# First queries through the casting queue, group 3 transposed by TensorE, part of a normalisation moved to ScalarE, and the last store in halves: a windowed attention with a SwiGLU block on one core

## The chip, the core and the metric

The kernel runs on one core of a Trainium2 chip. The metric is the device time of one execution in microseconds; the median of 14 executions of the kernel before is 250.9 us (249.39 to 252.73).

## What is computed

Batch 4, 8 heads, 768 positions, head size 64; 4 sink positions and a window of 128. The attention output, heads side by side (512 wide), goes through a gated feed-forward block of inner width 1536. All inputs and the output are float32 in HBM.

```python
scores = scale * np.matmul(q, k.transpose(0, 1, 3, 2))
keep = is_sink | in_window          # pos < 4, or 0 <= query - key < 128
scores = np.where(keep, scores, -1000000000.0)
a = softmax(scores)                 # exp over its row sum
x = np.matmul(a, v)                 # then (B, S, H*D) -> 3072 x 512
g = x @ w_gate
out = (g * sigmoid(g) * (x @ w_val)) @ w_out
```

## The kernel before, in words

**Groups and blocks.** The 3072 tokens are cut twice. Attention works in 12 groups g of 256 tokens, three for each batch entry. The feed-forward block works in 8 token blocks tb of 256 or 512 tokens: `SIZES = [256, 256, 256, 512, 512, 512, 512, 256]`. Groups 0, 1, 2 are blocks 0, 1, 2; groups 3 and 4 are block 3, and so on.

**Loading.** Keys, queries, values and weights are read through POOL's DMA queue, which casts float32 to bf16 on the way. POOL has eight completion semaphores for it and uses them in turn, so a DMA on POOL waits until the one eight places before it has landed. `load4(g)` (L96) loads a group with four tokens in a partition row, keys in partitions 0 to 63, queries in 64 to 127, one DMA each. `load1(g)` (L107) loads it with one token in a row, in four DMAs. The buffers `nat` are four. Group 0 has its own code: two casting DMAs for halves of the keys (L169), and the queries as float32 in four DMAs (L173), two each from ACT's and SP's queues, into staging tiles `st`.

**From tokens to columns.** The score matmuls need keys and queries with head size on the partitions. Groups below `NPE = 3` are transposed by PE (`transpose`, L257, matmuls with an identity of the same type; an ACT copy brings the keys and a DVE copy the queries from PSUM, L263). The others are transposed by two DMA transpositions on SP's queue (`cross_T`, L285), from `nat` to the tile kqT.

**One group's attention.** `step_S(g, p2)` does the scores of four heads (PE L323), exponentials on ACT (L330), and the mask by a DVE multiplication (L335). `step_K` does the sink scores for groups that aren't the first of their batch entry. `step_PV(g, j, hh)` does half of the heads of one 128-token tile j (PE L370) with a column of ones that gives the row sums, then a reciprocal (L375) and the product xn on DVE (L382); with `act` the product is made by four ACT operations (L378). `step_X(g, j)` transposes xn by PE (L406) into xT, evicted by DVE (L412) or ACT (L410). From group 5 on (`NXPE`) SP's DMA transposes xn instead (L388).

**The feed-forward units.** `gate(tb, f)` computes pg and pv (L434, eight matmuls of 256 columns or four of 512 each), tanh on ACT (L441), then u and ht on DVE (L447, L448). `down(tb, ts)` accumulates 12 matmuls (L462) for 128 tokens, evicts them on ACT with a factor of 0.5 (L466), and SP stores them (L468).

**The order** is written by hand. After a start for group 0, in which `warm(n)` fills PE with matmuls on zeros (L235), `weave(us, slots)` walks a list of feed-forward units and calls the attention steps that a table puts in each. In the first list, units 0 to 13 are the gates of blocks 0 and 1 and one down, 14 to 19 the gates of block 2, and 20 to 24 the remaining downs of blocks 0 to 2:

```python
us = [g0[0], (alone, 0, 0), *g0[1:4], *g1, *g0[4:6], downs(0)[0], *g2,
      downs(0)[1], *downs(1), *downs(2)]
```

Inside a gate unit the steps come between pg and pv. DVE work of a step is put off in a list `later` and issued by `flush` at the unit's end, or where the table says flush. Each engine works through its instructions in the order issued. T(g), Ss(g), K(g), PVs(g), Xs(g) in the table are the steps named above; C(g) is `cross_T(g)`, and T and C end by issuing the loads of group g + 4. `sinks(b)` copies the sink keys of a batch entry (L295) and builds its sink values (L300).

Of the kernel before, what the change touches and what calls it, by code (L numbers as in the profile page):

```python
# [8 lines left out]
FP32 = mybir.dt.float32  # L9
# [6 lines left out]
def kernel(  # L16
# [26 lines left out]
    SIZES = [256, 256, 256, 512, 512, 512, 512, 256]  # L43
    assert sum(SIZES) == NTOK and NG == 12 and S == 768
    OFF = [sum(SIZES[:i]) for i in range(len(SIZES))]
    NPE = 3
    NXPE = 5
    VS = 72
    FCH = [2, 2, 2, 2, 4]
# [30 lines left out]
    def bank(shape, dtype, name):  # L80
        return psum.tile(shape, dtype, tag="b", name=name)
# [4 lines left out]
    def four_tokens(src, g, hs):  # L86

        b, c = divmod(g, GC)
        return src[b, hs, c * 256:(c + 1) * 256].rearrange(
            "h (m r) d -> m h (r d)", r=4)  # L90

    def load4(g):

        x = natp.tile([P, H, 4 * D], BF16, tag="kq", name="kq")
        for i, src in ((0, k), (1, q)):
            nc.gpsimd.dma_start(  # L96
                x[64 * i:64 * (i + 1)], four_tokens(src, g, slice(0, H)))
        nat[g] = x

    def load1(g):  # L100

        b, c = divmod(g, GC)
        x = natp.tile([P, 2, 2, H * D], BF16, tag="kq", name="kq")
        for j in range(2):
            t0 = c * 256 + j * P
            for i, src in ((0, k), (1, q)):
                nc.gpsimd.dma_start(  # L107
                    x[:, j, i].rearrange("p (h d) -> p h d", d=D),
                    src[b, :, t0:t0 + P].rearrange("h m d -> m h d"))
        nat[g] = x  # L110
# [44 lines left out]
        ks = const.tile([P, NP2 * KS], BF16, tag=f"ks{b}", name="ks")  # L155
        kss.append(ks)


    nc.vector.memset(ident, 0.0)
    id32 = const.tile([P, P], FP32)  # L160
    nc.vector.memset(id32, 0.0)
    wm = const.tile([P, 512], BF16)
    nc.vector.memset(wm, 0.0)
    wake = const.tile([P, 1], FP32)
    nc.vector.memset(wake, 0.0)
    nat[0] = natp.tile([P, H, 4 * D], BF16, tag="kq", name="kq")
    for k2 in range(2):
        hs = slice(4 * k2, 4 * k2 + 4)
        nc.gpsimd.dma_start(nat[0][0:64, hs], four_tokens(k, 0, hs))  # L169
    first = []  # L170
    for p in range(NP2):
        st = opool.tile([P, 2, 4 * D], FP32, tag="ot", name="st")
        (nc.scalar, nc.sync)[p % 2].dma_start(  # L173
            st[64:P], four_tokens(q, 0, slice(2 * p, 2 * p + 2)))
        first.append(st)
    make_identity(nc, ident, nomemset=True)
    make_identity(nc, id32, nomemset=True)
    load_v(0)
    load_gate(0)

# [7 lines left out]
    for ks in kss:  # L188
        nc.vector.memset(ks, 0.0)
    nc.vector.memset(diag_h, 1.0)  # L190


    nc.gpsimd.iota(tq, [[1, P]], base=0, channel_multiplier=0,
                   allow_small_or_imprecise_dtypes=True)
    nc.gpsimd.iota(tk, [[0, 1]], base=0, channel_multiplier=1,
                   allow_small_or_imprecise_dtypes=True)
    dh = diag_h.rearrange("q (p h) -> q p h", h=2)
    nc.gpsimd.affine_select(
        out=dh, in_=dh, compare_op=ALU.is_ge, fill=0.0, base=0,
# [31 lines left out]
    def warm(n):  # L231

        ps = bank([P, 512], FP32, "wm")
        for _ in range(n):
            nc.tensor.matmul(ps, ident, wm, start=True, stop=True)  # L235

    def step_T(g, ph):

        if ph == 0:
            new_kq(g)  # L240
        own = lambda i, p: nat[g][:, 2 * p:2 * p + 2]
        transpose(g, ph, own, (ident, ident))

    def new_kq(g):
        kTs[g] = kqtp.tile([P, NP2, 256], BF16, tag="kT", name="kT")
        qTs[g] = kqtp.tile([P, NP2, 256], BF16, tag="qT", name="qT")

    def transpose(g, ph, rows, ids):


        pts = [bank([P, 2, 64, 4], FP32, "pt") for _ in range(2)]
        for p in range(2):
            for r in range(4):
                for h in range(2):
                    for i in range(2):
                        o = slice(64 * i, 64 * (i + 1))
                        nc.tensor.matmul(  # L257
                            pts[i][64 * h:64 * (h + 1), p, :, r],
                            rows(i, 2 * ph + p)[o, h, r * D:(r + 1) * D],
                            ids[i][o, o], start=True, stop=True)  # L260
        for i, (dst, copy) in enumerate(((kTs, nc.scalar.copy),
                                         (qTs, nc.vector.tensor_copy))):
            copy(out=dst[g][:, 2 * ph:2 * ph + 2],  # L263
                 in_=pts[i].rearrange("q a m r -> q a (m r)"))
# [42 lines left out]
    def step_S(g, p2):  # L307

        b, c = divmod(g, GC)
        if p2 == 0:  # L310
            e_t[g] = epool.tile([P, H, 512], BF16, tag="e", name="e")

        parts = [(2 * c, 0, 2, P), (2 * c + 1, 1, 1, 3 * P)]
        if c > 0:
            parts.insert(0, (2 * c - 1, 0, 1, 0))
        lo = 0 if c > 0 else P
        pss = [bank([P, 512], FP32, "s") for _ in range(4)]
        for pp in range(2):
            p = 2 * p2 + pp
            for t, j, n, col in parts:  # L320
                for h in range(2):
                    r = slice(h * D, (h + 1) * D)
                    nc.tensor.matmul(  # L323
                        pss[2 * pp + h][:, col:col + n * P], keys(b, t, r, p),
                        queries(g, r, p, j, n), start=True, stop=True)
        m = (mask if c > 0 else mask0).rearrange("q (o a) x -> q o (a x)", o=1)
        for pp in range(2):
            h0 = 4 * p2 + 2 * pp
            for h in range(2):
                nc.scalar.activation(  # L330
                    e_t[g][:, h0 + h, lo:512], pss[2 * pp + h][:, lo:512],
                    AF.Exp, scale=scale)

            def dve(e=e_t[g][:, h0:h0 + 2, lo:512]):
                nc.vector.tensor_tensor(  # L335
                    e, e, m[:, :, lo:512].broadcast_to([P, 2, 512 - lo]), op=ALU.mult)
            later.append(dve)
# [80 lines left out]
    def gate(tb, f, attn):  # L418
# [30 lines left out]
            hts[tb][:, f:f + two].rearrange("p a n -> p (a n)"), u, pv, op=ALU.mult)  # L449
        flush()  # L450

    def down(tb, ts, attn):
        po = bank([P, DM], FP32, "pd")
        n = DFC // 4
        at = {}
        for i, a in enumerate(attn):
            at.setdefault(DFC * (i + 1) // (len(attn) + 1), []).append(a)
        for f in range(DFC):
            for a in at.get(f, []):
                a()  # L460
                flush()
            nc.tensor.matmul(  # L462
                po, hts[tb][:, f, ts * P:(ts + 1) * P], wos[f // n][:, f % n],
                start=(f == 0), stop=(f == DFC - 1))
        ot = opool.tile([P, DM], FP32, tag="ot", name="ot")
        nc.scalar.activation(ot, po, AF.Copy, scale=0.5)  # L466
        r0 = OFF[tb] + ts * P
        nc.sync.dma_start(out[r0:r0 + P], ot)  # L468
# [9 lines left out]
    def downs(tb):  # L478
        return [(down, tb, t) for t in range(SIZES[tb] // P)]
# [56 lines left out]


    new_kq(0)
    warm(10)
    for ph in range(2):  # L540
        transpose(0, ph, lambda i, p: first[p] if i else nat[0][:, 2 * p:2 * p + 2],
                  (ident, id32))
    build_masks()
    step_S(0, 0)
    warm(2)
    step_S(0, 1)
# [16 lines left out]
    for i in range(4):  # L563
        load_out(i)
    for g in (3, 4):
        load1(g)
        load_v(g)


    g0, g1, g2 = gates(0), gates(1), gates(2)  # L570
    us = [g0[0], (alone, 0, 0), *g0[1:4], *g1, *g0[4:6], downs(0)[0], *g2,
          downs(0)[1], *downs(1), *downs(2)]
    weave(us, slots(
        (0, T(1)), (1, Ss(1) + [K(1)]), (3, PVs(1) + [flush]),
        (4, [A(step_X, 1, 0), A(step_X, 1, 1, True), flush]),
        (8, T(2)), ((9, 10), Ss(2)), (10, [K(2)]), (10, C(3)),
        (11, PVs(2)[:2] + [flush]), (12, PVs(2)[2:] + [flush]),
        (13, [A(step_X, 2, 0), A(step_X, 2, 1, True), flush]), (13, C(4)),
        ((16, 17), Ss(3)), (18, sinks(1)), ((18, 18, 19, 19), PVs(3)),
        (20, Xs(3)), ((20, 21), Ss(4)), (21, [K(4)]),  # L580
        (22, C(5)), ((22, 22, 23, 23), PVs(4)), (24, Xs(4))))

    def pair(ga, gb, sh=0):
        s = sh
# [46 lines left out]
```

## Time and profile before

| | |
|---|---|
| median of 14 executions | 250.9 us |
| the profiled execution | 250.02 us |
| its span | 248.3 us |
| PE busy | 234.0 us (94%) |
| DVE busy | 161.1 us (65%) |
| ACT busy | 110.9 us (45%) |
| POOL busy | 68.7 us (28%) |
| software DMA queue, share of 16 engines' span | 69.2% |
| hardware DMA queue of SP | 25.3% |
| last matmul ends, last eviction ends | 244.4 us, 245.1 us |

The times in the views are microseconds from the start of the span. A line of a timeline gives start, length, engine, source line, operation, output<-inputs and a count; a bracket gives the idle time of the engine just before it and what ended it. A busy PE is not always PE doing needed work: the filler matmuls wm count as busy. Transfers show twice, as the issuing instruction on POOL or SP and as DMA time until the data have landed.

### The profile page before, as it was taken

Reading aid. Unit: us, or ns where it says so; the run is one execution under the profiler, and the core shown is the slowest. Engines: PE = TensorE matmul, PEld = TensorE weight load, DVE = VectorE, ACT = ScalarE, POOL = GpSimd, SP = SyncE. Lnnn points to the kernel's source line nnn. Section 1 sums busy time; section 2 is a strip of 40 time slices with the busy share of each in tenths; the row PEclk is TensorE's granted clock in tenths of the full one; section 3 lists DMA queues with packets and bytes.
Section 4 is the critical chain, followed back from the end, with each engine's and each line's share of the span. In section 5 each row is a group of like instructions: output and inputs, shape, how many; then the busy total and the mean of one; then the engine's idle time right before and its main releaser. Section 6 shows DMA issues by size and latency. Waiting matters only on the chain.

```text
span 248.3 us, 5061 instructions
## 1 busy us (share of the span) xinstructions
PE 234.0 (94%) x2011; PEld 133.4 (54%) x2011; DVE 161.1 (65%) x339; ACT 110.9 (45%) x219; POOL 68.7 (28%) x90
## 2 busy tenths in 40 slices
PE   4979899999699999999999999999999999999993
PEld 1557687777545444544445454445454445488441
DVE  2478978948954388892398981298980389878000
ACT  2478338437162266542665711555612662232121
POOL 8965373954694088005200000000000000000000
PEclk9999999999999999999999999999999999999999
DMA  7999999999999999759960264600244200200122
GB/s 135 170 185 199 202 192 183 145 122 153 180 154 198 164 243 156 38 67 171 207 110 0 44 87 124 173 3 1 48 82 127 84 3 0 42 3 0 61 111 84
DMA packets 102775, 27.63 MB, mean 111 GB/s; under 512 B 89952, under 2 KB 99680, under 8 KB 102752
## 3 DMA queue, kind: packets, MB, share of 16 engines
q0 software_dynamic: 71936, 13.90, 69.2%
q1 hardware_dynamic: 30528, 13.15, 25.3%
q10 hardware_dynamic: 288, 0.26, 0.5%
q8 instruction: 16, 0.26, 0.4%
q14 instruction: 7, 0.06, 0.1%
HBM read 28.34 MB, written 6.29 MB: 139 GB/s over the span
## 4 chain that ended last, share of the span: by engine, by line
PE 65%; DMA 17%; DVE 9%; POOL 4%; issue 2%; ACT 0%; DVEq 0%; POOLq 0%; ACTq 0%; SPq 0%
PE pd L462 24%; PE pv L434 18%; PE pg L434 16%; DMA kq<-in_k_dram 5%; DMA kq<-in_q_dram 5%; DMA kqT<-kq 4%; PE o L370 4%; DMA wv<-in_moe_w_val_dram 3%; PE s L323 3%; DVE ht L448 3%; DVE e L335 2%; DVE u L447 2%; DVE xn L382 1%; POOL kq L107 1%; POOL va L123 1%
## 5 line engine op out<-in xcount | busy, mean ns | idle before, releaser
L434 PE MATMUL pv<-xT,wv 128*128 128x256 bf16 (+1 forms) x384 | 74.3, 326 | 1.3 <-DVE ht L448 1.1
L434 PE MATMUL pg<-xT,wg 128*128 128x256 bf16 (+1 forms) x384 | 74.2, 326 | 0.8 <-DVE xT L412 0.6
L441 ACT ACTIVATE th<-pg 128x512 f32<-128x512 f32 x72 | 43.4, 606 | 64.8 <-PE pg L434 64.4
L447 DVE SCALAR_TENSOR_TENSOR u<-th,pg 128x512 bf16<-128x512 f32 x72 | 49.1, 682 | 31.1 <-ACT th L441 30.7
L462 PE MATMUL pd<-wo,ht 128*128 128x512 bf16 x288 | 66.5, 379 | 0.0
L448 DVE TENSOR_TENSOR ht<-u,pv 128x512 bf16<-128x512 bf16 x72 | 49.5, 687 | 10.2 <-PE pv L434 3.3
L434 PEld LDWEIGHTS <-wg 128*128 128x128 bf16 x384 | 37.3, 98 | 27.0 <-issue 1.0
L330 ACT ACTIVATE e<-s 128x512 bf16<-128x512 f32 (+1 forms) x96 | 46.0, 581 | 6.7 <-PE s L323 6.6
L434 PEld LDWEIGHTS <-wv 128*128 128x128 bf16 x384 | 34.7, 98 | 21.2 <-issue 3.1
L462 PEld LDWEIGHTS <-ht 128*128 128x128 bf16 x288 | 26.8, 98 | 28.8 <-issue 0.3
L466 ACT ACTIVATE ot<-pd 128x512 f32<-128x512 f32 x24 | 14.5, 603 | 51.1 <-PE pd L462 51.1
L335 DVE TENSOR_TENSOR e<-e,mask 128x1024 bf16<-128x1024 bf16 (+1 forms) x48 | 29.1, 641 | 4.2 <-ACT e L330 3.9
L107 POOL DMA_DIRECT2D kq<-in_k_dram x18 | 16.1, 896 | 30.6 <-DMA kqT<-kq 27.7
L123 POOL DMA_DIRECT2D va<-in_v_dram x24 | 21.5, 907 | 7.8 <-DMA kq<-in_q_dram 2.9
L382 DVE TENSOR_TENSOR xn<-o,rcp 128x256 bf16<-128x256 f32 x46 | 19.5, 424 | 1.6
L370 PEld LDWEIGHTS <-e 128*128 128x128 bf16 x352 | 16.4, 98 | 7.2 <-DVE e L335 2.0
L370 PE MATMUL o<-va,e 128*128 128x65 bf16 x352 | 18.0, 193 | 1.2 <-DVE e L335 1.1
L107 POOL DMA_DIRECT2D kq<-in_q_dram x18 | 16.2, 899 | 3.4 <-DMA wo<-in_moe_w_out_dram 1.6
L375 DVE RECIPROCAL rcp<-o 128x4 f32<-128x4 f32 x48 | 8.4, 176 | 9.6 <-PE o L370 9.6
L323 PE MATMUL s<-kqT 64*128 64x256 bf16 (+1 forms) x192 | 10.4, 238 | 0.5 <-DMA kqT<-kq 0.5
L235 PE MATMUL wm<-wm,ident 128*128 128x512 bf16 x19 | 7.1, 513 | 3.1 <-POOL ident masks.py:199 3.1
L323 PEld LDWEIGHTS <-kqT 64*128 64x128 bf16 x192 | 6.2, 94 | 6.8 <-issue 6.5
(55 smaller groups left out, 87.1 us busy)
## 6 DMA issues: line engine op xcount, KB each, us to landing
out_dram<-ot SPq DMA_DIRECT2D x24, 256.0 KB
va<-in_v_dram POOLq DMA_DIRECT2D x24, 128.0 KB, 7.7
kq<-in_k_dram POOLq DMA_DIRECT2D x20, 128.0 KB, 6.8
kq<-in_q_dram POOLq DMA_DIRECT2D x18, 128.0 KB, 6.8
wo<-in_moe_w_out_dram POOLq DMA_DIRECT2D x4, 384.0 KB, 12.3
wg<-in_moe_w_gate_dram POOLq DMA_DIRECT2D x4, 256.0 KB, 7.9
wv<-in_moe_w_val_dram POOLq DMA_DIRECT2D x4, 256.0 KB, 8.5
kq<-in_k_dram POOLq DMA_DIRECT2D x2, 256.0 KB, 9.6
```

The source lines that it names most:

```text
L107: nc.gpsimd.dma_start(x[:, j, i].rearrange("p (h d) -> p h d", d=D), src[b, :, t0:t0 + P].rearrange("h m d -> m h d"))
L123: nc.gpsimd.dma_start(va[:, j, :, 0:D], v[b, :, t0:t0 + P].rearrange("h m d -> m h d"))
L323: nc.tensor.matmul(pss[2 * pp + h][:, col:col + n * P], keys(b, t, r, p), queries(g, r, p, j, n), start=True, stop=True)
L330: nc.scalar.activation(e_t[g][:, h0 + h, lo:512], pss[2 * pp + h][:, lo:512], AF.Exp, scale=scale)
L335: nc.vector.tensor_tensor(e, e, m[:, :, lo:512].broadcast_to([P, 2, 512 - lo]), op=ALU.mult)
L370: nc.tensor.matmul(o, l, r, start=(i == 0), stop=(i == len(mms) - 1), skip_group_check=True)
L382: nc.vector.tensor_tensor(xns[g, j][:, 256 * hh:256 * (hh + 1)].rearrange("p (h d) -> p h d", h=4), po[:, :, 0:D], rcp.broadcast_to([P, 4, ...
L434: nc.tensor.matmul(ps[:, i * n:(i + 1) * n], ws[fi][:, c, fo * P:(fo + 1) * P], x[:, 0:n // P, c], start=(c == 0), stop=(c == DMC - 1))
L441: nc.scalar.activation(th, pg, AF.Tanh, scale=0.5)
L447: nc.vector.scalar_tensor_tensor(u, th, 1.0, pg, op0=ALU.add, op1=ALU.mult)
L448: nc.vector.tensor_tensor(hts[tb][:, f:f + two].rearrange("p a n -> p (a n)"), u, pv, op=ALU.mult)
L462: nc.tensor.matmul(po, hts[tb][:, f, ts * P:(ts + 1) * P], wos[f // n][:, f % n], start=(f == 0), stop=(f == DFC - 1))
```

## The change

Group 0's queries are loaded like its keys, by casting DMAs, with keys and queries in two halves of four heads each that alternate on the queue. The float32 staging tiles and the float32 identity go. Fillers use the zero tile as weights instead of the identity, and the first run of them has 8 in place of 10. The two iotas that the masks need move up on POOL, ahead of the first value and weight loads, and the masks are built between the two transpositions of group 0. Group 3 is loaded by `load4` and transposed by PE (`NPE = 4`), in unit 14; the table is rearranged around it: C(4) in unit 12 for 13, S(3) in 15 and 16 for 16 and 17, PV(3) in 17 and 18 for 18 and 19, C(5) in 18 for 22, S(4) in 19 and 20 for 20 and 21, PV(4) in 21 and 22 for 22 and 23, X(3) behind S(4) in unit 20. In group 1, the products xn of tile j = 1 are made by ACT. The last 128 tokens go through `last_down`: two halves of 256 columns, the first evicted by ACT and stored from ACT's queue, the second evicted by DVE and stored from SP's.

```diff
-    NPE = 3
+    NPE = 4
...
-    def load4(g):
+    def load4(g, parts=1):
         x = natp.tile([P, H, 4 * D], BF16, tag="kq", name="kq")
-        for i, src in ((0, k), (1, q)):
-            nc.gpsimd.dma_start(
-                x[64 * i:64 * (i + 1)], four_tokens(src, g, slice(0, H)))
+        n = H // parts
+        for h0 in range(0, H, n):
+            for i, src in ((0, k), (1, q)):
+                nc.gpsimd.dma_start(
+                    x[64 * i:64 * (i + 1), h0:h0 + n],
+                    four_tokens(src, g, slice(h0, h0 + n)))
...
-    for k2 in range(2):
-        hs = slice(4 * k2, 4 * k2 + 4)
-        nc.gpsimd.dma_start(nat[0][0:64, hs], four_tokens(k, 0, hs))
-    first = []
-    for p in range(NP2):
-        st = opool.tile([P, 2, 4 * D], FP32, tag="ot", name="st")
-        (nc.scalar, nc.sync)[p % 2].dma_start(
-            st[64:P], four_tokens(q, 0, slice(2 * p, 2 * p + 2)))
-        first.append(st)
+    load4(0, 2)
     make_identity(nc, ident, nomemset=True)
-    make_identity(nc, id32, nomemset=True)
+    nc.gpsimd.iota(tq, ...)
+    nc.gpsimd.iota(tk, ...)
     load_v(0)
     load_gate(0)
...
-            nc.tensor.matmul(ps, ident, wm, start=True, stop=True)
+            nc.tensor.matmul(ps, wm[:, 0:P], wm, start=True, stop=True)
...
+    def last_down(tb, ts):
+        n = DFC // 4
+        r0 = OFF[tb] + ts * P
+        for i, copy, eng in ((0, nc.scalar.mul, nc.scalar),
+                             (1, nc.vector.tensor_scalar_mul, nc.sync)):
+            c = slice(i * DM // 2, (i + 1) * DM // 2)
+            po = bank([P, DM // 2], FP32, "pd")
+            for f in range(DFC):
+                nc.tensor.matmul(
+                    po, hts[tb][:, f, ts * P:(ts + 1) * P], wos[f // n][:, f % n, c],
+                    start=(f == 0), stop=(f == DFC - 1))
+            ot = opool.tile([P, DM], FP32, tag="ot", name="ot")
+            copy(ot[:, c], po, 0.5)
+            eng.dma_start(out[r0:r0 + P, c], ot[:, c])
...
-    warm(10)
-    for ph in range(2):
-        transpose(0, ph, lambda i, p: first[p] if i else nat[0][:, 2 * p:2 * p + 2],
-                  (ident, id32))
+    warm(8)
+    transpose(0, 0)
     build_masks()
+    transpose(0, 1)
...
     for g in (3, 4):
-        load1(g)
+        (load4 if g < NPE else load1)(g)
...
+    p1 = [A(step_PV, 1, j, hh, j == 1) for hh in range(2) for j in range(2)]
     weave(us, slots(
-        (0, T(1)), (1, Ss(1) + [K(1)]), (3, PVs(1) + [flush]),
+        (0, T(1)), (1, Ss(1) + [K(1)]), (3, p1 + [flush]),
         (4, [A(step_X, 1, 0), A(step_X, 1, 1, True), flush]),
-        (8, T(2)), ((9, 10), Ss(2)), (10, [K(2)]), (10, C(3)),
-        (11, PVs(2)[:2] + [flush]), (12, PVs(2)[2:] + [flush]),
-        (13, [A(step_X, 2, 0), A(step_X, 2, 1, True), flush]), (13, C(4)),
-        ((16, 17), Ss(3)), (18, sinks(1)), ((18, 18, 19, 19), PVs(3)),
-        (20, Xs(3)), ((20, 21), Ss(4)), (21, [K(4)]),
-        (22, C(5)), ((22, 22, 23, 23), PVs(4)), (24, Xs(4))))
+        (8, T(2)), ((9, 10), Ss(2)), (10, [K(2)]),
+        (11, PVs(2)[:2] + [flush]), (12, PVs(2)[2:] + [flush]), (12, C(4)),
+        (13, [A(step_X, 2, 0), A(step_X, 2, 1, True), flush]),
+        (14, T(3)), ((15, 16), Ss(3)), (16, sinks(1)), ((17, 17, 18, 18), PVs(3)),
+        (18, C(5)), ((19, 20), Ss(4)), (20, Xs(3) + [K(4)]),
+        ((21, 21, 22, 22), PVs(4)), (24, Xs(4))))
```

More of the change, by code (lines that the diff above doesn't have):

```diff
@@ L159 @@
     nc.vector.memset(ident, 0.0)
-    id32 = const.tile([P, P], FP32)
-    nc.vector.memset(id32, 0.0)
     wm = const.tile([P, 512], BF16)
@@ L165 @@
     nc.vector.memset(wake, 0.0)
-    nat[0] = natp.tile([P, H, 4 * D], BF16, tag="kq", name="kq")
-    for k2 in range(2):
-        hs = slice(4 * k2, 4 * k2 + 4)
-        nc.gpsimd.dma_start(nat[0][0:64, hs], four_tokens(k, 0, hs))
-    first = []
-    for p in range(NP2):
-        st = opool.tile([P, 2, 4 * D], FP32, tag="ot", name="st")
-        (nc.scalar, nc.sync)[p % 2].dma_start(
-            st[64:P], four_tokens(q, 0, slice(2 * p, 2 * p + 2)))
-        first.append(st)
+    load4(0, 2)
     make_identity(nc, ident, nomemset=True)
-    make_identity(nc, id32, nomemset=True)
+    nc.gpsimd.iota(tq, [[1, P]], base=0, channel_multiplier=0,
+                   allow_small_or_imprecise_dtypes=True)
+    nc.gpsimd.iota(tk, [[0, 1]], base=0, channel_multiplier=1,
+                   allow_small_or_imprecise_dtypes=True)
     load_v(0)
@@ L190 @@
     nc.vector.memset(diag_h, 1.0)
[L193 to L196, printed above, removed]
     dh = diag_h.rearrange("q (p h) -> q p h", h=2)
@@ L240, in step_T @@
             new_kq(g)
-        own = lambda i, p: nat[g][:, 2 * p:2 * p + 2]
-        transpose(g, ph, own, (ident, ident))
+        transpose(g, ph)
     def new_kq(g):
@@ L246, in new_kq, with transpose @@
         qTs[g] = kqtp.tile([P, NP2, 256], BF16, tag="qT", name="qT")
-    def transpose(g, ph, rows, ids):
+    def transpose(g, ph):
         pts = [bank([P, 2, 64, 4], FP32, "pt") for _ in range(2)]
@@ L258, in transpose @@
                             pts[i][64 * h:64 * (h + 1), p, :, r],
-                            rows(i, 2 * ph + p)[o, h, r * D:(r + 1) * D],
-                            ids[i][o, o], start=True, stop=True)
+                            nat[g][o, 4 * ph + 2 * p + h, r * D:(r + 1) * D],
+                            ident[o, o], start=True, stop=True)
         for i, (dst, copy) in enumerate(((kTs, nc.scalar.copy),
@@ L450, in gate @@
         flush()
+    def last_down(tb, ts):
[12 more added lines that the diff above has]
+            eng.dma_start(out[r0:r0 + P, c], ot[:, c])
     def down(tb, ts, attn):
+        if OFF[tb] + (ts + 1) * P == NTOK:
+            return last_down(tb, ts)
         po = bank([P, DM], FP32, "pd")
```

## The prediction

> **What bounds the kernel now.** I read the page's busy shares first, then the waits of PE, then PE's and ACT's timelines around each wait, then the chain of waits, and the DMA queues last. All times are us from the span's start.
>
> ```profile
> PE 234.0 (94%) x2011; PEld 133.4 (54%) x2011; DVE 161.1 (65%) x339; ACT 110.9 (45%) x219; POOL 68.7 (28%) x90
> ...
> PE   4979899999699999999999999999999999999993
> ```
>
> PE is busy in 94% of the span, from slice 4 on almost wholly. Matmuls that PE no longer issues, or waits of PE that go, are worth their length; other engines count only where PE waits for them.
>
> ```profile
> PE wm L235 <- POOL ident masks.py:199: 3.1, 1, 3.1
> PE px L406 <- DVE xn L382: 2.6, 3, 2.2
> ...
> PE pg L434 <- DVE xT L412: 0.6, 1, 0.6
> PE s L323 <- DMA kqT<-kq: 0.5, 1, 0.5
> ```
>
> These waits (total, times, longest) are most of what can be won without taking work off PE: the start, one of 2.2, and one of 0.5 on a DMA.
>
> ```profile
> 3.14 4.45 PE L235 MATMUL wm<-wm,ident 128*128 128x512 bf16 x10 [3.14 <-POOL ident masks.py:199]
> ...
> 10.03 0.50 PE L323 MATMUL s<-qT,kT 64*128 64x256 bf16 x8
> 10.46 0.60 PE L235 MATMUL wm<-wm,ident 128*128 128x512 bf16 x2
> ...
> 16.95 1.03 PE L434 MATMUL pg<-xT,wg 128*128 128x256 bf16 x8 [0.24 <-ACT xT L410]
> ...
> 57.27 0.51 PE L323 MATMUL s<-kqT 64*128 64x256 bf16 x8 [0.50 <-DMA kqT<-kq]
> ...
> 68.19 0.28 PE L406 MATMUL px<-ident,xn 128*128 128x128 bf16 x2 [2.17 <-DVE xn L382]
> ```
>
> In PE's timeline the busy figure misleads before 16.95: wm is filler, and the real work there is a chain of latencies. First scores start at 10.03, the first gate matmul at 16.95. ACT sets that stretch:
>
> ```profile
> 10.62 3.18 ACT L330 ACTIVATE e<-s 128x384 bf16<-128x384 f32 x8
> 13.82 0.93 ACT L378 ACTIVATE xn<-o,rcp 128x64 bf16<-128x64 f32 x4
> ```
>
> The eight exponentials run without a gap (no bracket), and the normalisation of the first group follows them at once. So 16.95 moves with the start of S(0,0).
>
> ```profile
> 35.14 11.24 DMA kq<-in_q_dram
> 46.39 0.02 SPq L285
> 46.41 0.03 issue
> 46.44 10.69 DMA kqT<-kq
> ```
>
> In the chain of waits group 3 passes a casting load of 11.24 and a DMA transposition of 10.69, and PE is reached at 57.27.
>
> **The change part by part.** The sum is against the profiled execution: 250.02, its span 248.3 and 1.7 around it.
>
> *Start.* It removes four loads of f32 queries (two issued by ACT, two by SP), the f32 identity, two fillers, and the f32 transpositions, whose group counts 64 passes on PE, for which 32 bf16 matmuls come. It adds two casting DMAs on POOL. POOL's order becomes k, q, k, q halves at 1.32, 2.0, 2.7, 3.4 (0.63 to 0.76 each in the L169 rows), identity at about 4.1, the two iotas (0.28 + 0.18), then V and the first weights, issued 1.5 later than now. Fillers no longer wait for the identity: from 1.4, 8 x 0.43 = 3.4, to 4.8.
>
> When does the last query half land? Landing of the two L169 loads now: 3.8 and 5.0 after issue, while 0.52 MB of f32 queries share the DMA engines. Without them four halves of 131 KB written follow each other at about 0.75 (k1 to q2, 256 KB each, land 1.1 to 1.9 apart), so 4.9, 5.6, 6.4, 7.2. Bounds: 6.7 (issue-limited) and 9.0 (each as slow as the present second half, 2.0 apart, at the end). I take 7.2, nearest to the saturated rows. T(0,1) then runs to 8.1 (32 bf16 matmuls; 64 take 1.02 at full speed, so 0.5 to 0.9), S(0,0) starts at 8.1 instead of 10.03, and ACT's exponentials at about 8.75 instead of 10.62: 1.9 earlier. The masks move between the two transpositions and cost nothing there: 1.29 on DVE, beside the wait for the second halves.
>
> Two things take some back. First the clock. The row: fillers of 512 columns take 634 ns to 7.5 and 379 ns at 10.46, with start-to-start 0.43 and 0.22; the speed changes at 8.65, inside 5.5 of unbroken PE work. The Trainium skill, "TensorE: Matmul & The Clock Gate", Part 1 (HAM clock gate), says that PE runs at half clock until one free-running window of about 3.4 us has been busy. That speaks against this change: 3.4 of filler, then gaps for the q halves, fills no window except by luck of its phase. By the row alone (fast after 4 to 5.5 of PE work in sum) S(0,0) runs fast and the cost is 0; by the rule PE stays slow until about 12, and S, four or more fillers and PV at half speed cost some 0.3 beyond what ACT hides, up to 1.5 if it stays slow to the first gates. I take 0.3. (The page's clock row is 9 throughout and doesn't show this.) Second, the casting queue carries 0.26 MB more, so its later loads land about 1.3 later (bounds 0.5 and 2.5) until group 3. q of group 1 lands at 15.3 now and is used at 17.91; the gate weights 2 and 3 land at 20.5 and 24.1 and are used at 23.35 and 26.99. Slack 2.6 to 2.9, of which the later landing takes 1.3: about 1.3 of the earlier start survives. So **start -1.3** (bounds -2.2 and 0).
>
> *Group 1's normalisation.* Two of four xn (0.42, 0.34 when back to back) leave DVE: 0.7 off it at 26.6. ACT gets 2 x 0.93 behind the second reciprocal: 27.35 to 29.2. Behind it on ACT waits the tanh of unit 4 (28.07 now, then 29.2), and px of the second half waits on PE until 29.2 instead of 28.4. PE's pg of unit 5, which now waits 0.56 for DVE's xT until 30.62, gets it at about 30.45 from ACT. The wait changes its name, **-0.1** (bounds -0.3 and +0.6).
>
> *Group 3.* Removes four casting loads (0.88 to 0.91 each on POOL, landing 0.9 apart), replaced by two (0.69 to 0.73; group 2's land 1.2 apart), and two DMA transpositions from SP (1.33 and 3.41). It adds 64 matmuls (1.02, as 17.91 to 18.93 for group 1), two ACT evictions (1.07) and two DVE casts (1.29). Group 3's q lands by about 47 and T(3) comes at about 51: no wait. **PE +1.0.** The wait of 0.50 at 57.27 goes. The wait of 2.17 at 68.19 goes too: it is X(3) right behind PV(3) while DVE is 2 late, and X(3) now stands after S(4,1), a unit and more behind PV(3). **-2.7.** The score, PV and X work is the same, only earlier.
>
> What is late next? S(4,0), moved into unit 19. From pg of unit 14 at 52.23: eleven gate halves x 0.87 = 9.6, T 1.0, two S(3) halves 0.9, four PV 0.7, so 64.4, less the 1.4 gained before: 63.0. Group 4's transpositions are moved past nothing on SP but the missing two: the last output weights land at 43.0 now, so 44.3; 2.4 for group 3, 1.9 for its V, 1.8 for k and q of group 4's first half make 50.4. The pair of group 3 took 44.73 to 57.13 = 12.4 from first issue to landing, so 62.8. Level: I book 0.5 (bounds 0 and 5). DVE has in units 14 to 19 six u+ht x 1.29, 1.3 casts, 1.9 + 1.3 masks, 1.05 sinks and 2.2 for PV = 15.5 against 13.6 of PE; but the same pattern for group 2 (T, S, S, PV, PV at 35.9 to 50.7) left DVE 1.5 behind and PE unhindered, and the down units behind are light on DVE. I book 0.3 (0 to 1.5). **+0.8.** On POOL group 8's loads now go before group 7's and wait for group 4's transposition; group 7 then lands near 78, wanted near 105: nothing. Group 6's loads, which wait until 57.69 for group 3's transposition, wait for PE instead.
>
> *Last tile.* PE does 24 x 256 columns for 12 x 512: the same 2.6 (8 of 256 take 0.87 in the gates). ACT's half is done beside the second half's matmuls.
>
> ```profile
> 244.53 0.60 ACT L466 ACTIVATE ot<-pd 128x512 f32<-128x512 f32 x1 [1.99 <-PE pd L462]
> ...
> SPq L626 <- DMA out_dram<-ot: 1.4, 1, 1.4
> ```
>
> The eviction behind the last matmul falls from 0.60 to about 0.42 (xn, 128x256 from PSUM on DVE), and its store is 128 KB; the windows of DMA show 256 KB flowing from 246.0 to 246.73, so half saves 0.36. **-0.55** (bounds -0.8 and 0).
>
> Sum: -1.3 - 0.1 + 1.0 - 2.7 + 0.8 - 0.55 = -2.85, about -2.8. The profiled execution becomes 247.2. It lies 0.9 below the median of 250.9, so the median becomes 248.1.
>
> **The rivals.** *The start gives nothing* (0.20): the last query half lands at 9.0, PE is slow to the first gates, later loads pin the rest. For: the second half now takes 5.0. Against: its competitor goes. Then 249.4. *All covers hold* (0.15): last half at 6.7, no new wait at S(4), tail 0.8: -2.2 - 0.3 - 1.7 - 0.8 = -5.0, 245.9. *Slower: group 4's DMA transposition is late* (0.13). One place: S(4,0) in unit 19, which now stands a unit later, at 69.93, some 6 after the hardware queue's packets end (63 to 64). For: the casting queue no longer stops at 55 to 57 for group 3, so it shares the engines all the time; those transpositions stretch from 1.3 to 4.4 on SP in such company. Against: the 12.4 already includes it, and 0.52 MB at the 0.09 MB per us seen from 57 to 63 is 6. Landing at 68 costs 5 on PE, in place of the 0.5: -2.8 + 4.5 = +1.7, 252.6. A wait of 3.3, a landing at 66.3, eats the rest of the gain; from 67.1 on the kernel is measurably slower. That the edit doesn't take effect is excluded: the instruction order shows T(3) on PE and no transposition of group 3 on SP.
>
> **How the numbers follow.** Likeliest (0.52): 248.1, alone 247.2 to 249.2. 0.3% is 0.75 and about what a measurement tells from no change. Faster (below 250.15): 0.52 + 0.15 + half of the dead start 0.10 = 0.77; same: the other half, 0.10; slower: 0.13. The range of 246.3 to 250.5 leaves out the slow case and the best edge.
>
> **What would show it.** S(0,0) at 8 to 9 and pg of unit 0 at 15.2 to 16.5; slow fillers (634 ns) past 10 for the clock; no kqT wait at S(3), none of 2 at X(3); S(4,0) near 63 with a wait under 1 named kqT; a last eviction of 0.4. Wrong if S(0,0) starts after 9.5, if PE waits for wg, wv or kq between 15 and 30 for over 1, or for kqT over 3.3 in unit 19.

## The result, and the profile after

The changed kernel takes 248.66 us (median of 10 executions, 248.06 to 249.58) against 251.01 for the kernel before on the same chip (48 executions). The ratio is 0.9913, with a 95% interval of 0.9887 to 0.9939: faster by 0.9%. The prediction was 248.1. Ratios and their intervals, here and below, are estimated from executions in the fast state alone and are not the quotients of the medians beside them. The profiled execution of after took 248.64 with a span of 246.6, so the span is 1.7 shorter than before's, and the time 1.4.

The page of after, busy shares:

```profile
PE 234.8 (95%) x2053; PEld 134.5 (55%) x2053; DVE 161.2 (65%) x339; ACT 113.5 (46%) x229; POOL 67.6 (27%) x89
```

PE is busy 0.8 longer than before, though the span is shorter: its idle time fell from 14.3 to 11.8. The waits of PE (total, times, longest) say which are left:

```profile
PE pt L246 <- DMA kq<-in_k_dram: 1.4, 1, 1.4
PE wm L225 <- DVE wake L165: 1.3, 1, 1.3
PE pv L423 <- DVE ht L437: 1.1, 3, 0.4
PE pg L423 <- PE pd L469: 0.8, 1, 0.8
...
PE pt L246 <- DMA kq<-in_q_dram: 0.6, 1, 0.6
```

Before's wait of 2.17 at X(3) and its 0.50 for kqT are gone. New are 1.4 and 0.6 at the start, for the halves of keys and queries (the first fillers ended while the loads were still under way), and 0.8 booked to "PE pd", which is something else, as will be seen. PE's timeline of after at the places that the prediction stepped through:

```profile
7.38 0.24 PE L246 MATMUL pt<-ident,kq 64*64 64x64 bf16 x1 [1.38 <-DMA kq<-in_k_dram]
8.23 0.64 PE L246 MATMUL pt<-ident,kq 64*64 64x64 bf16 x31 [0.61 <-DMA kq<-in_q_dram]
8.80 0.70 PE L312 MATMUL s<-qT,kT 64*128 64x256 bf16 x8
...
16.03 1.03 PE L423 MATMUL pg<-xT,wg 128*128 128x256 bf16 x8 [0.24 <-ACT xT L399]
...
29.17 1.03 PE L423 MATMUL pg<-xT,wg 128*128 128x256 bf16 x8
...
51.74 1.09 PE L246 MATMUL pt<-ident,kq 64*64 64x64 bf16 x64
...
64.21 0.21 PE L312 MATMUL s<-kqT,kT 64*128 64x128 bf16 x1 [0.34 <-DVE u L436]
...
65.00 1.03 PE L423 MATMUL pv<-xT,wv 128*128 128x256 bf16 x8 [0.41 <-DVE ht L437]
...
118.94 1.02 PE L423 MATMUL pg<-xT,wg 128*128 128x512 bf16 x4 [0.81 <-PE pd L469]
```

Subtracting the same marks of before gives the account:

| stretch | before | after | change | booked |
|---|---|---|---|---|
| first gate matmul (pg of unit 0) starts | 16.95 | 16.03 | -0.92 | -1.3 |
| from there to pg of unit 5 | 13.67 | 13.14 | -0.53 | -0.1 |
| to pg of unit 14 | 21.61 | 21.60 | 0 | 0 |
| to the first gate of block 3 (84.34 / 82.11) | 32.11 | 31.34 | -0.77 | -0.9 |
| to the first gate of block 4 (120.28 / 118.94) | 35.94 | 36.83 | +0.89 | 0 |
| to the last whole eviction (241.94 / 240.23) | 121.66 | 121.29 | -0.37 | 0 |
| to the end of the span | 6.36 | 6.37 | 0 | -0.55 |
| time outside the span | 1.7 | 2.0 | +0.3 | 0 |

These are single executions, and the first row moves by itself: over four profiles of kernels with the old start that matmul starts at 15.89 to 17.67 (mean 16.85), over seven with the new one at 15.34 to 16.61 (mean 15.95). The last row does not move: time less span is 1.99 to 2.09 in all executions of after, 1.66 to 1.84 in those of before. No view of the profile shows what lies there.

### The profile page after: what moved, and what is told of

It reads as the page before. It is cut to its first block, busy times and chain, and to the rows that moved or that the text cites. A ratio compares the mean times of both kernels' runs of the same rounds, so it can differ in the third digit from the quotient of the medians.

```text
span 246.6 us, 5140 instructions
## 1 busy us (share of the span) xinstructions
PE 234.8 (95%) x2053; PEld 134.5 (55%) x2053; DVE 161.2 (65%) x339; ACT 113.5 (46%) x229; POOL 67.6 (27%) x89
## 4 chain that ended last, share of the span: by engine, by line
PE 78%; DVE 10%; ACT 5%; DMA 3%; issue 2%; POOL 1%; DVEq 0%; ACTq 0%; POOLq 0%
PE pd L469 24%; PE pv L423 22%; PE pg L423 20%; PE o L359 5%; PE s L312 3%; DVE ht L437 3%; ACT e L319 3%; DVE e L324 2%; DVE u L436 2%; DMA kq<-in_q_dram 2%; PE pt L246 1%; DVE xn L371 1%; PE wm L225 1%; PE px L395 1%; DMA out_dram<-ot 1%
## 5 line engine op out<-in xcount | busy, mean ns | idle before, releaser
L469 PE MATMUL pd<-wo,ht 128*128 128x512 bf16 x276 | 63.7, 379 | 0.0
L469 PEld LDWEIGHTS <-ht 128*128 128x128 bf16 x276 | 25.8, 98 | 27.5 <-issue 0.2
L473 ACT ACTIVATE ot<-pd 128x512 f32<-128x512 f32 x23 | 13.7, 597 | 51.2 <-PE pd L469 51.2
L110 POOL DMA_DIRECT2D kq<-in_k_dram x16 | 14.2, 888 | 27.0 <-DMA kqT<-kq 22.2
L371 DVE TENSOR_TENSOR xn<-o,rcp 128x256 bf16<-128x256 f32 x44 | 18.7, 424 | 1.5
L110 POOL DMA_DIRECT2D kq<-in_q_dram x16 | 14.3, 893 | 5.6 <-DMA va<-in_v_dram 2.7
L252 DVE CAST qT<-pt 128x512 bf16<-128x512 f32 x8 | 5.2, 687 | 8.9 <-PE pt L246 8.9
L312 PE MATMUL s<-kqT 64*128 64x128 bf16 (+1 forms) x168 | 9.4, 238 | 0.0
```

What stands on the lines that cost most here:

```text
L110: nc.gpsimd.dma_start(x[:, j, i].rearrange("p (h d) -> p h d", d=D), src[b, :, t0:t0 + P].rearrange("h m d -> m h d"))
L312: nc.tensor.matmul(pss[2 * pp + h][:, col:col + n * P], keys(b, t, r, p), queries(g, r, p, j, n), start=True, stop=True)
L371: nc.vector.tensor_tensor(xns[g, j][:, 256 * hh:256 * (hh + 1)].rearrange("p (h d) -> p h d", h=4), po[:, :, 0:D], rcp.broadcast_to([P, 4, ...
L469: nc.tensor.matmul(po, hts[tb][:, f, ts * P:(ts + 1) * P], wos[f // n][:, f % n], start=(f == 0), stop=(f == DFC - 1))
```

## The experiments

### One part of the change at a time

Four kernels take before and make one part of the change each: the new start; the ACT products in group 1; group 3 on PE with its table; the last tile in halves. Their edits are the parts of the diff above.

**The new start alone.**

```diff
-    nat[0] = ...; first = [...]   # f32 queries on ACT's and SP's queues
+    load4(0, 2)
...
-    warm(10)
+    warm(8)
```

> The kernel before with the start alone (casting queue for the first queries, 8 fillers, masks between the transpositions). Theory from the changed kernel's trace: pg of unit 0 at 16.0 and the gain kept, about -0.9 us. Prediction's size: -1.3. Rival (dead start): the later landing of the weights takes it back, 0 or slower.

Measured: 255.88 (252.92 to 257.17, 6 executions), ratio 1.0146 (1.0094 to 1.0198). This part, which gains in the change, alone makes the kernel slower by 1.5%. The chain of waits of this kernel and PE's timeline:

```profile
37.86 10.82 DMA kq<-in_q_dram
48.68 0.02 SPq L274
48.70 0.03 issue
48.73 11.43 DMA kqT<-kq
```

```profile
55.48 1.04 PE L423 MATMUL pg<-xT,wg 128*128 128x256 bf16 x8
60.30 0.51 PE L312 MATMUL s<-kqT 64*128 64x256 bf16 x8 [3.79 <-DMA kqT<-kq]
60.74 1.89 PE L423 MATMUL pv<-xT,wv 128*128 128x256 bf16 x8
62.42 1.89 PE L423 MATMUL pg<-xT,wg 128*128 128x256 bf16 x8
...
64.68 1.05 PE L423 MATMUL pv<-xT,wv 128*128 128x256 bf16 x8
```

Group 3's queries land at 48.7; before they landed at 46.4. The added 0.26 MB on the casting queue pushes them back 2.3 (the prediction took 1.3 for such loads), the two DMA transpositions behind them end at 60.2, and PE, which stood there at 56.8 in before, is idle for 3.79. The two gate halves after that pause take twice their time. The windows of the trace show why (stretch, length, busy times of PE, PEld, DVE, ACT and POOL, granted clock, DMA share, GB/s):

```profile
60.00:62.00 2.00, 1.70 (x15) 1.20 (x16) 0.00 (x0) 1.34 (x4) 0.88 (x1) 0.69 1.78 156
62.00:64.00 2.00, 2.00 (x11) 1.37 (x9) 1.33 (x3) 0.30 (x1) 1.15 (x2) 0.50 3.12 143
```

The granted clock is 0.50 behind the pause. So the transposition of group 3 is a wall, a place where the DMA engines and not PE set the time: whoever gets there earlier waits longer. The wall and the slow halves make 3.29 + 1.76 = 5.05 of the 6.0 by which the span grew. Two more waits belong to the account. The first gate came 1.61 earlier than in before, but at T(1) PE stood 1.12 for group 1's queries, which also came later. And ahead of block 4 there is this wait:

```profile
PE pg L423 <- issue: 1.7, 1, 1.7
```

That place is taken up below.

**The ACT products alone.**

```diff
+    p1 = [A(step_PV, 1, j, hh, j == 1) for hh in range(2) for j in range(2)]
...
-        (3, PVs(1) + [flush]),
+        (3, p1 + [flush]),
```

> The kernel before with group 1's tile 1 normalised on ACT alone. Theory from the trace: PE reaches pg of unit 5 0.5 us earlier after unit 0, so about -0.5. Prediction's size: -0.1. Rival: without the new start the tanh behind the ACT products is late, +0.3 or worse.

Measured: 250.34, ratio 0.9962 (0.9936 to 0.9988): faster by 0.4%. Its timeline at unit 5 and at the wall:

```profile
29.02 1.03 PE L434 MATMUL pg<-xT,wg 128*128 128x256 bf16 x8
...
56.60 0.51 PE L323 MATMUL s<-kqT 64*128 64x256 bf16 x8 [1.45 <-DMA kqT<-kq]
```

The pg of unit 5 has lost its wait: 13.13 from pg of unit 0, as in after (13.14) and not 13.67 as in before. But the wait for kqT is 1.45 for 0.50. Not all of that is this part's doing: in this execution the first gate came 1.06 earlier than in before's, and the kernel with the last tile alone, which is before up to there, waits 0.88. PE's clock takes its share too. Behind the wait of 2.17 at X(3), which before has as well, this execution shows:

```profile
68.00:70.00 2.00, 2.00 (x9) 1.03 (x8) 0.72 (x3) 0.00 (x0) 1.64 (x3) 0.50 2.47 154
```

Before's profiled execution keeps the clock at 1.00 there. So one profile doesn't show how much of the 0.53 passes the wall; the ratio says that the gain is not all lost.

**Group 3 on PE alone.**

```diff
-    NPE = 3
+    NPE = 4
...
-        (10, C(3)), ... (13, C(4)), ((16, 17), Ss(3)), ...
+        (12, C(4)), ... (14, T(3)), ((15, 16), Ss(3)), ...
```

> The kernel before with group 3 loaded four tokens a row, transposed by PE, and the new table (without ACT products in group 1). Theory from the trace: the stretch from pg of unit 14 to block 3's first gate shrinks by 0.8, of which 0.8 may be lost again in front of block 4: -0.8 to 0. Prediction's size: -0.9. Rival: the rearranged table is what matters in the DVE queue, and the kernel gains 1.5 or more because nothing waits at S(4).

Measured: 251.08, ratio 0.9994 (0.9968 to 1.0019): no difference. In this profile the wait ahead of block 4, which after books to "PE pd", is named otherwise:

```profile
PE pg L434 <- DMA xT<-xn: 0.7, 1, 0.7
```

It is a wait for a DMA transposition. It comes with this part, but not with this part only: the start alone has it too, as 1.67 of "issue". In this execution the clock is 0.50 from 16 to 18, at the end of the old start, where before's has 1.00.

**The last tile alone.**

```diff
+        if OFF[tb] + (ts + 1) * P == NTOK:
+            return last_down(tb, ts)
```

> The kernel before with the last tile in two halves alone. Theory from the trace: 0, since ACT's queue takes 1.95 us to issue the first half, whose data then go last. Prediction's size: -0.55. Rival: ACT's queue has been used at the start in this kernel (queries), so its issue is short here and -0.5 shows.

Measured: 251.14, ratio 0.999 (0.9965 to 1.0015). From the start of the last whole eviction to the end of the span it takes 6.02 (242.18 to 248.2), 0.34 less than before. But the time outside the span is 2.03 to 2.22 in all its executions, for 1.66 to 1.84 in those of before: what the tail gains is lost where the profile doesn't look. In after the same edit gains nothing inside the span either. (With group 3 on PE alone the time outside is 2.00 to 2.11, with the start or the ACT products alone 1.66 to 1.83.)

The four ratios are 1.0146, 0.9962, 0.9994 and 0.999. Added, they make +0.9%; together the parts give -0.9%.

**The start and group 3 together.**

> The kernel before with the new start and group 3 by PE, without ACT products in group 1 and without the halves. Theory: the new start costs only because group 3's DMA transposition comes later; with group 3 on PE the two together give what the four give less the 0.5 of the products: 249.2, no kqT wait at S(3). Rival (the start alone is slower for another cause, such as q of group 1 landing late): still over 251.

Measured: 249.24, ratio 0.993 (0.9908 to 0.9952). The start that costs 1.5% alone is worth 0.6% once the wall is gone: S(3) runs at 55.25 without a wait. The gap between what the two give together (-0.7%) and their sum (+1.4%) is where the parts depend on each other. The wait ahead of block 4, 0.81, is there without the other two parts.

### The tail

In after, the tail runs so (ACTq and SPq are the issues of DMAs):

```profile
240.23 0.60 ACT L473 ACTIVATE ot<-pd 128x512 f32<-128x512 f32 x1 [2.04 <-PE pd L469]
241.82 0.38 ACT L454 ACTIVATE ot<-pd 128x256 f32<-128x256 f32 x1 [0.99 <-PE pd L450]
242.24 1.95 ACTq L455 DMA_DIRECT2D out_dram<-ot  x1
242.86 0.42 DVE L454 TENSOR_SCALAR ot<-pd 128x256 f32<-128x256 f32 x1 [14.39 <-DMA out_dram<-ot]
243.31 0.33 SPq L455 DMA_DIRECT2D out_dram<-ot  x1
```

ACT spends 1.95 on one issue, SP 0.33, and the half that was ready a microsecond earlier is stored last: data of ACT's queue flow from 244.5 to 245.5, those of SP's from 244.0 to 244.8. In the kernel with the last tile alone ACT has issued two loads at the start, and there:

```profile
243.91 0.36 ACTq L466 DMA_DIRECT2D out_dram<-ot  x1
```

Two experiments on after look for the reason. In one, both halves are stored by SP:

```diff
-        for i, copy, eng in ((0, nc.scalar.mul, nc.scalar),
+        for i, copy, eng in ((0, nc.scalar.mul, nc.sync),
```

> The changed kernel with the first half of the last tile stored from SP's queue instead of ACT's. Theory: ACT's issue of 1.95 us, the first DMA that ACT issues in this kernel, makes the first half's data go last; from SP's queue the span ends about 0.5 us earlier, 248.1 against 248.66. Rival (the fixed wait behind the last store sets the end): no change.

Measured: 248.35, ratio 0.9882 (0.9848 to 0.9916). The tail is 5.72 (241.68 to 247.4), 0.65 shorter than in after. In the other, ACT still stores the half, but issues one small load of constants at 1.65, at the program's start, too:

```diff
-        nc.sync.dma_start(                                # vcf
+        (nc.scalar if h == 0 else nc.sync).dma_start(     # vcf
```

> The changed kernel with the first of the eight small sink-value loads issued by ACT instead of SP. Theory: ACT's 1.95 us for the last tile's first store is the price of the first DMA that ACT issues; with an early one it is about 0.36, as in the kernel that has the halves alone, and the span ends 0.3 to 0.6 earlier behind the same last matmul. Rival (an instruction fetch at that place): the 1.95 stays.

Measured: 247.98, ratio 0.9893 (0.9841 to 0.9946). Its store, late in the program:

```profile
242.07 0.38 ACTq L455 DMA_DIRECT2D out_dram<-ot  x1
```

The tail is 5.75 (240.35 to 246.1). So an issue at this place isn't always dear, and after's loss of the tail gain is a side effect of its other parts. That 1.95 is the price of a first DMA is not shown, and two things speak against it. ACT's first DMA here, the load at 1.65, takes 0.57. And ACT is late before it issues anything: it begins to evict the half 1.84 after PE begins that half's matmuls, in after and also in the kernel in which ACT issues no DMA, against 1.55 here and 1.56 with the last tile alone. A rival is a read of instructions, which in after falls into the long issue, between 242.6 and 242.7:

```profile
q14 instruction: 1, 0.01, 4.6%
```

Here that queue reads between 241.3 and 241.4, 0.7 ahead of the store. The early load may have moved the read, so these runs don't tell the two apart. The medians of both kernels lie inside or just below after's range of 248.06 to 249.58, so a gain in time isn't shown; the shorter tails are.

### The wait ahead of block 4

The theory: group 11's casting loads, which in after start at 111.41 on POOL (114.28 in before), share the DMA engines with the DMA transposition of group 6's xT, issued at 111.68 (113.91 in before). Leaving those six loads out takes away the company (group 11 then computes with group 10's tiles):

```diff
+        if g + 4 == 11:
+            nat[11], vas[11] = nat[10], vas[10]
```

> The changed kernel without the six casting loads of group 11 (its tiles are those of group 10, so the last 256 tokens are computed from other data). Theory: the wait of 0.81 in front of block 4's first gate is for the DMA transposition of group 6's last xn, slowed by these loads, which start 3 us earlier than before; without them the wait goes and the span falls by 0.8. Rival (the wait is for PE's or DVE's own work, as the trace names PE): the wait stays.

Measured: 247.77, ratio 0.986 (0.9828 to 0.9893). The windows of after first, then of this kernel, in the same columns as above:

```profile
111.00:115.00 4.00, 4.00 (x27) 1.97 (x26) 1.21 (x4) 0.60 (x1) 3.60 (x5) 1.00 0.92 131
115.00:119.00 4.00, 3.19 (x16) 1.31 (x15) 0.00 (x0) 1.19 (x2) 1.67 (x2) 1.00 1.87 180
```

```profile
111.00:115.00 4.00, 3.95 (x26) 1.95 (x26) 1.14 (x4) 0.60 (x1) 0.00 (x0) 1.00 0.49 131
115.00:119.00 4.00, 4.00 (x23) 1.73 (x22) 0.00 (x0) 1.25 (x3) 0.00 (x0) 1.00 0.34 131
```

PE is busy for 3.19 of the four microseconds in after and for all of them here. The 0.81 is gone, and the first gate of block 4 starts at 117.88 without a bracket. "PE pd" was only the name of what PE had finished before it stood. Of the 0.9 that the median is under after's, 0.3 isn't the wait's: the time outside the span is 1.68 to 1.74 here.

But before has these loads beside the transposition too, and no wait. The difference is which goes out first. Before, then after:

```profile
113.91 2.50 SPq L388 DMA_TRANSPOSE xT<-xn  x2
114.28 0.88 POOL L107 DMA_DIRECT2D kq<-in_k_dram  x1 [15.84 <-DMA kqT<-kq]
```

```profile
111.41 0.88 POOL L110 DMA_DIRECT2D kq<-in_k_dram  x1 [10.54 <-DMA kqT<-kq]
111.68 2.57 SPq L377 DMA_TRANSPOSE xT<-xn  x2
```

In the three profiles in which the loads begin behind the transposition (by 0.37 in before, 0.58 with the ACT products alone, 0.93 with the last tile alone) PE doesn't wait. In the nine in which they begin 0.23 to 0.29 ahead of it, PE waits 0.55 to 1.67. No run moves the order alone, so this is read from the profiles and not shown by an experiment.

### The start and the clock

Five more fillers between the two transpositions of group 0 keep PE going while it waits for the second halves:

```diff
     transpose(0, 0)
+    warm(5)
     build_masks()
```

> The changed kernel with 5 more fillers between the two transpositions of group 0. Theory: PE is then busy without a break from 1.3 on, its clock is released near 8 instead of 12, S(0,0) and the fillers behind it run at full speed and pg of unit 0 comes 0.3 to 0.7 earlier. Rival (the fillers delay the second transposition by more than the clock is worth, or ACT hides the slow clock): 0 or slower by up to 0.5.

Measured: 248.6, ratio 0.9887 (0.9857 to 0.9917); no gain over after. Two windows of after, and the same ones of this kernel:

```profile
9.00:10.00 1.00, 1.00 (x10) 0.26 (x6) 0.63 (x1) 1.00 (x3) 1.00 (x3) 0.50 1.30 155
10.00:11.00 1.00, 1.00 (x10) 0.39 (x8) 0.56 (x1) 1.00 (x4) 1.00 (x2) 0.50 1.25 161
```

```profile
9.00:10.00 1.00, 0.85 (x10) 0.38 (x10) 0.33 (x2) 1.00 (x4) 1.00 (x3) 1.00 1.30 148
10.00:11.00 1.00, 0.85 (x7) 0.27 (x5) 0.79 (x2) 1.00 (x4) 1.00 (x2) 1.00 1.30 158
```

In after the granted clock is 0.50 from 9 to past 12, with the fillers it is 1.00. From S(0,0) to pg of unit 0 it takes 7.23 in after and 6.92 here, and in three kernels with these fillers that gate starts at 15.36 to 15.39. The new start's own pauses thus cost about 0.3 in this execution. How often the clock is lost shows in the second eight scores, S(0,1): with both halves of the last tile stored by SP, and with the start alone,

```profile
10.66 0.82 PE L312 MATMUL s<-qT,kT 64*128 64x256 bf16 x8 [0.36 <-ACT e L319]
```

```profile
9.39 0.50 PE L312 MATMUL s<-qT,kT 64*128 64x256 bf16 x8
```

Of the seven profiles with the new start and without these fillers, five have 0.82 there and two 0.50; from S(0,0) to the gate it takes 7.03 to 7.61 in the five and 6.92 in the two. The granted clock alone would mislead: in the first of these two kernels it reads 1.00 from 7 to 13, while the scores take the slow time. The 0.67 won at the start is lost at the next wall:

```profile
64.48 0.34 PE L312 MATMUL s<-kqT 64*128 64x256 bf16 x4 [1.08 <-DMA kqT<-kq]
```

Here PE comes to S(4) ahead of group 4's DMA transposition. One more kernel loads group 4's keys and queries ahead of group 3's values to move that wall:

```diff
-    for g in (3, 4):
-        (load4 if g < NPE else load1)(g)
-        load_v(g)
+    for g in (3, 4):
+        (load4 if g < NPE else load1)(g)
+    for g in (3, 4):
+        load_v(g)
```

> The changed kernel with the 5 fillers, and group 4's keys and queries loaded before group 3's values. Theory: with the fillers alone the 0.7 won at the start was lost at S(4) to group 4's transposition (wait 1.08), which lands two V loads (1.9) sooner here: no kqT wait, 0.7 to 1.0 below the changed kernel, 247.8. Rival (the hardware queue only shares with other casting loads, or V of group 3 is late at PV(3)): the same time, a wait for va or kqT.

Measured: 248.47, ratio 0.9901 (0.9872 to 0.993). The wait for kqT goes, S(4) waits for DVE alone (0.35). The profile has PE waiting 0.60 for group 1's queries instead, and 0.56 remains ahead of block 4. The wall is moved; no gain in time is shown.

### DVE in unit 19

Moving `sinks(1)` from unit 16 to unit 20 was to take DVE work from in front of S(4):

```diff
-        (16, sinks(1)),
...
-        (20, Xs(3) + [K(4)])
+        (20, Xs(3) + sinks(1) + [flush, K(4)])
```

> The changed kernel with the sink keys and values of the second batch entry made in unit 20 instead of 16: 1.05 us of DVE work leaves the overfull stretch. Theory: the two waits of PE on DVE in unit 19 (0.34 and 0.41) go, -0.7. Rival (DVE's backlog only moves to unit 20 and delays the sink scores or PV(4) there): 0.

Measured: 249.61, ratio 0.9929 (0.9907 to 0.9951), not better than after. The two DVE waits in unit 19 go, and this comes:

```profile
70.41 0.29 PE L335 MATMUL pk<-kqT,ks 128*32 128x256 bf16 x4 [1.33 <-DVE ks L284]
```

The sink scores now wait for their keys. The 0.75 of DVE waits was the cheaper place.

### A better version

The last kernel takes the fillers, group 4's early loads, both stores by SP, and a cheap way to hold group 11's loads until the transposition of xT is done: POOL copies one column of xT first.

```diff
+    def load_11():
+        nc.gpsimd.tensor_copy(out=late, in_=xTs[4][:, 3, 0, 0:1])
+        load1(11)
+        load_v(11)
```

> As the last, with both halves of the last tile stored from SP's queue, and group 11's loads held back on POOL until group 6's last xn has been transposed (a one-column copy on POOL waits for it). Theory: 0.65 at the end and 0.81 before block 4 more, about 246.4. Rival (the waits only move: another DMA in the next block, or the store): 247.5 or more.

Measured: 247.33 (246.41 to 248.43, 6 executions), ratio 0.9865 (0.9819 to 0.9911), against 0.9913 (0.9887 to 0.9939) for after: ahead of both kernels in the median, though the two intervals overlap, so that it is faster than after isn't shown. It stays 0.9 short of the 246.4 that was expected; the profiled execution, 246.41, is the fastest of the six. There is no wait ahead of block 4, and POOL's timeline gives the time when the transposition has landed:

```profile
114.84 0.19 POOL L604 COPY late<-xT 128x1 bf16<-128x1 bf16 x1 [14.66 <-DMA xT<-xn]
```

That is 3.8 after its issue at 111.00. In after it was issued at 111.68, and PE waited for it until 118.94, 7.3 later.

## Why the prediction was right

The time was within 0.6 of the forecast, but that is in part luck. The terms were summed on profiled executions, and there the change is -1.4 (250.02 to 248.64) for a booked -2.8. The medians differ by 2.35, because before's profiled execution lay 1.0 under its median and after's at its own. The prediction carried before's distance over to after.

**What held.** The mechanism was right: PE bounds the kernel, and only its idle times and its order count. S(3) no longer waits, the wait of 2.17 at X(3) is gone, and T(3) took 1.02 from start to start (51.74 to 52.76) for a booked 1.0. Group 4's transposition was booked to be issued at 50.4 and to land at 62.8. It was issued at 50.49, and POOL's next loads, which wait for that tile to come free, start at 62.55, so it had landed then; the slower rival, which needed 67.1 or later, had 4.5 to go. The mark of group 3 came to -0.77 for a booked -0.9. Inside that term two sizes were off: kqT cost 0 instead of 0.5, and DVE 0.34 + 0.41 = 0.75 instead of 0.3.

**The start, -0.92 for -1.3.** Two sizes were off. "I take 7.2" for the last query half was the first: PE waits for it until 8.23, so it lands a full microsecond later, still inside the bounds (6.7 and 9.0). S(0,0) moved by 1.23 and not 1.9. The second was the later landing of the loads behind, 1.3, which with the slack of 2.6 at T(1) set the -1.3. POOL's issue that waits for group 1's queries goes out at 17.17, for 15.53 in before: 1.6 later, which leaves 1.0. With the start alone they land 2.4 later than the prediction's 15.3, and PE stands for them. The clock's 0.3 was right in size for this execution and is 0.1 to 0.7 over the five that lost it; the prediction weighed it against 0, which is what two of seven show. The Trainium skill ("TensorE: Matmul & The Clock Gate", Part 1) lets the outcome depend on the phase of a free-running window; the spread over the seven agrees with that.

**Group 1's normalisation, -0.53 for -0.1.** The mis-sized term is "29.2": ACT's instructions were added one after another at their full length. ACT starts them closer. Its timeline in after:

```profile
28.00 0.65 ACT L430 ACTIVATE th<-pg 128x512 f32<-128x512 f32 x1
28.48 0.64 ACT L399 COPY xT<-px 128x512 bf16<-128x512 bf16 x1
```

An instruction of 0.65 is followed by the next after 0.48. The eviction was done in time, the pg of unit 5 doesn't wait at all, and the two px wait 0.18 each.

**The last tile, 0 for -0.55.** The step costed the eviction and the amount of data, and took the issue on ACT's queue to cost what an issue costs on SP's. It cost 1.95 for 0.33, which the other parts of the change bring about; why is open. With SP the tail gives -0.65, so the rest of the term was sound inside the span. The sum kept 1.7 for the time around the span; it became 2.0.

**Block 4, +0.89 for 0.** "Nothing" was said of the order of group 7's and 8's loads, with a view only to when those groups are wanted. What changed was the place of group 11's loads: against the transposition of xT, which PE needs at once, they moved from 0.37 behind to 0.27 ahead. The loads' own deadline was safe; their company was not looked at.

**What stays open.** Of the -0.37 behind block 4, a wait of 0.41 on DVE at 171.70 of before, which after lacks, accounts for its size; why it left was not tried. Nor is it known what the 0.3 outside the span is. And before's distance of 1.0 between profile and median goes with the clock. Of 108 executions of before, the 28 with a mean granted clock of 0.996 or more have a median of 249.87, the 49 from 0.989 to 0.995 one of 251.31, the 31 below one of 252.28; the profiled one, at 0.999, is of the first kind. In after the first two kinds have 248.79 and 248.64. So the profile that the sum was made on doesn't show what most executions of before lose, and after's executions don't show that loss. The slow stretches behind X(3) and at the end of the old start, each seen in one profile of a kernel that has that place from before, are candidates; how much each costs was not measured.

## What to carry to other kernels

Parts of a change don't add up across a wall: where PE waits for a DMA chain, an earlier arrival is worth little, and if it delays that chain it costs more than it could gain (the start: +1.5% alone, -0.6% with the wall gone), so find the next DMA-timed wait behind each gain before booking it. When loads move earlier, ask what else is on the DMA engines at their new time and which goes out first, and not only whether they are in time. When an edit changes what an engine has issued before, look at the length of its last issue. And before a sum made on one profile is set against a median, look how the executions spread and by what.

## What the runs showed of the hardware

- ACT's one store, late in the program, took 1.94 to 1.99 to issue in five kernels in which ACT issues no other DMA, and 0.36 and 0.38 in two in which it does. ACT's load at 1.65 took 0.57, the stores on SP 0.33. The cause is open.
- A pause of 3.79 on PE was followed by a granted clock of 0.50 to 0.69 for some 3.5 us (gate halves of 1.82 and 1.68 in the chain of waits, for 0.87), in the kernel with the start alone. A wait of 2.17 was followed by 0.50 in one kernel and by 1.00 in another.
- At the program's start, fillers of 3.5 us with pauses of 0.8 to 1.4 and 0.4 to 0.7 behind them left the second eight score matmuls at 0.82 in five profiles and at 0.50 in two; with five more fillers in the first pause they took 0.50 in all three. The granted clock read 1.00 in two of the five with 0.82.
- Casting loads that go out just ahead of two DMA transpositions lengthen them: 7.3 from issue until PE could go on in after, where the loads began 0.27 ahead, and 3.8 from issue to landing with the loads held back. Where they began 0.37 behind, PE could go on within 6.4.
